# Attention and a gated MLP in one kernel on one core: q loaded with six tokens a partition, single-head scores at the start, a halved last store, and a new order

## The chip, the cores and the metric

The kernel runs on one core of a Trainium2 chip. The core has five engines that each work through a queue of their own in order: TensorE (PE in the profile, with PEld for its weight loads), VectorE (DVE), ScalarE (ACT), GpSimd (POOL) and SyncE (SP), which here only issues transfers. Sixteen DMA engines move the data. The engines wait for each other through semaphores. The metric is the time of one execution in device microseconds; lower is better.

## The reference

Grouped-query attention, whose output goes straight into a gated MLP with a spatial product. B = 8 batches, 16 q heads, 4 kv heads, 384 tokens, head size 64.

```python
scores = scale * np.matmul(q, k.transpose(0, 1, 3, 2))     # k, v repeated for 4 q heads each
attn = np.exp(scores - max) / sum
x = (attn @ v) -> (8, 384, 1024)
h = np.maximum(x @ w_in, 0.0)                              # 1024 -> 1024
u, v = h[..., :512], h[..., 512:]
v_n = (v - mean) / sqrt(var + 1e-6)                        # over the 512
v_s = w_spatial @ v_n (over tokens) + b_spatial
out = (u * v_s) @ w_out                                    # 512 -> 1024, float32
```

## The kernel before

All products run in fp16. The whole work is cut into pieces, and `lay_out` makes an operation of each: a cost, what it waits for, which buffers it uses, and the code that emits it. `Plan.run` goes through time with these costs and fixes the order in which each engine gets its instructions and which PSUM bank or SBUF slot a buffer takes. TensorE's order is written out by hand as words (`RAMP`, `PATTERN` for batches 2 to 7, `TAIL`); the order of the other engines follows from the plan. `LOADS` is the order of the first loads, and `CASTS` says which engine casts which of them to fp16.

The words, with b for the batch and gp for a pair of kv heads:

- `T.q.b.gp.t`, `T.k`, `T.ws`: transposes by TensorE (L425), for batches 0 and 1 and the spatial weights; VectorE copies the result to qT, kT or wsT (L389). From batch 2 on q and k are turned by DMA (L411).
- `S.b.n`: one tile of scores for a pair of kv heads, two products of 64 rows and 512 columns that run side by side (L595). ScalarE takes the exponential of both, 128 x 1024, into aT (L601). There are 18 such tiles a batch.
- `SM`: the sums of the exponentials (L634, with a matrix of ones). VectorE first adds the three key tiles (L620 and L623, two additions for each query tile), except in batch 0, where TensorE adds them. ScalarE makes the reciprocal by a logarithm and an exponential (L639, L642).
- `X`: the exponentials times v (L634); VectorE scales it into xT (L677, in batch 0 L728). Batch 0 does this in two groups of query tiles, the first alone and the other two together (`GROUPS`).
- `V.b.st`: x times the second half of w_in; relu, then statistics and normalisation on VectorE (L762, L763, L784), with ScalarE's square root in between (L773, L774).
- `SP`: the spatial product; VectorE adds the bias (L802).
- `U.b.m`: x times the first half of w_in; VectorE takes the relu and multiplies (L882). In batch 0 U goes by the groups of X too, with uT in between (L843, L856, L865).
- `O.b.c`: the output product, six chunks of 128 x 512 a batch. `OCOPY` says which engine copies the chunk from PSUM (L387 on ScalarE, L389 on VectorE). SyncE then stores a row block of 128 x 1024, in the last batch each 128 x 512 (L915, L922).
- `D`: a product of zeros that nobody reads. The words of before have none.

A product in a gap with sums or X is cut into four column strips of 32 (L358, mode C); otherwise it is whole (L354, mode F). Scores are a third mode. SyncE issues every load and store; a load waits for a free slot (six of `st32` for q, k, v; four of `big` for weights and for output) and for the transfer eight places ahead of it.

Partition p holds tokens 3p, 3p + 1 and 3p + 2 of each head, so that a load of q brings runs of 768 bytes:

```python
return x.rearrange("i (p t) d -> p i (t d)", t=NST)
dst = lambda tt=tt: e.out[b].rearrange("(p t) d -> p t d", t=NST)[:, tt, :]
```

Of the kernel before, what the change touches and what calls it, by code (L numbers as in the profile page):

```python
# [11 lines left out]
FP32 = mybir.dt.float32  # L12
# [33 lines left out]
class Plan:  # L46
# [13 lines left out]
    LOADING = 42.0  # L60

# [96 lines left out]
    def run(self, ahead):  # L158
# [17 lines left out]
        while left:  # L176
            progress = True
            while progress:
                progress = False
                for e in engines:  # L180
# [7 lines left out]
                    for o in ready:  # L188
# [8 lines left out]
                        if e == "PE":  # L197
                            t = self.fetch(o, t)
                            cost = self.clocked(o, t)
                        if o.lock:  # L200
                            t = max(t, locked)
                            locked = t + o.cost
# [52 lines left out]
    "T.q.0.0.1 T.k.0.0 T.q.0.0.0 S.0.8 S.0.1 S.0.2 S.0.6 S.0.0 T.k.0.1 T.q.0.1.0 S.0.5 T.q.0.1.2 "  # L255
    "T.q.0.1.1 S.0.4 S.0.3 S.0.7 T.q.0.0.2 S.0.9 SM.0.1.0.0 SM.0.0.0.0 S.0.16 T.ws.0 S.0.17 "
    "T.ws.1 S.0.15 T.q.1.0.2 T.q.1.0.1 S.0.12 S.0.10 T.q.1.0.0 T.k.1 S.0.11 S.0.14 X.0.1.0.0 "
    "X.0.0.0.0 S.1.0 S.1.4 X.0.1.1.1 S.1.6 X.0.1.1.0 S.0.13 SM.0.1.1.0 T.q.1.1.2 S.1.3 T.q.1.1.1 "
    "T.q.1.1.0 SM.0.0.1.0 S.1.1 S.1.5 X.0.0.1.1 X.0.0.1.0 V.0.0 S.1.16 S.1.2 S.1.8 V.0.2 V.0.1 "
    "S.1.7 S.1.10 S.1.9 U.0.0.0 U.0.1.1 SP.0.3 SP.0.2 S.1.13 SP.0.0 S.1.11 SP.0.1 X.1.0.1.0 "  # L260
    "S.1.15 S.1.12 S.1.17 U.0.1.0 S.1.14 X.1.0.0.0 X.1.0.0.1 SM.1.0.0 O.0.1 X.1.1.0.0 SM.1.0.1 "
    "SM.1.1.0 O.0.0 X.1.1.0.1 X.1.0.1.1"
)
PATTERN = (
    "SM.-1.1.1 S.0.3 O.-2.2 S.0.0 S.0.1 S.0.4 X.-1.1.1.1 X.-1.1.1.0 O.-2.1 O.-2.3 S.0.7 S.0.2 "
    "S.0.6 O.-2.4 V.-1.1 S.0.5 S.0.8 S.0.10 V.-1.2 V.-1.0 S.0.15 S.0.17 S.0.9 O.-2.5 X.0.0.0.0 "
    "SM.0.0.0 U.-1.2 U.-1.1 SP.-1.2 S.0.13 S.0.16 SP.-1.1 SP.-1.0 SP.-1.3 U.-1.3 S.0.12 S.0.14 "
    "S.0.11 U.-1.0 X.0.0.1.0 SM.0.0.1 X.0.0.1.1 O.-1.0 X.0.0.0.1 SM.0.1.0 X.0.1.0.0 X.0.1.0.1"
)
TAIL = (  # L270
    "SM.7.1.1 X.7.1.1.1 X.7.1.1.0 O.6.4 O.6.2 V.7.0 V.7.2 V.7.1 U.7.0 U.7.2 O.6.5 O.6.3 SP.7.1 "
    "SP.7.0 U.7.1 SP.7.3 SP.7.2 U.7.3 O.6.1 O.7.5 O.7.1 O.7.3 O.7.2 O.7.4 O.7.0"
# [3 lines left out]
def words():  # L276
# [21 lines left out]
GROUPS = ((0,), (1, 2))  # L298
PIECE = {1: 0.195, 2: 0.342, 3: 3 * (S / 2400.0 + 0.0025)}
OCOPY = ("ACT", "ACT", "DVE", "DVE", "ACT", "DVE")  # L300
LOADS = (
    "0q1", "0q0", "0k0", "0q3", "0k1", "0q2", "ws", "wi12", "1q1", "wo2", "wi01", "wi10", "1q0",
    "1k", "wi11", "0v", "wi13", "wi02", "1q3", "wi00", "wi03", "wo3", "wo1", "1q2", "1v", "wo0",
)
CASTS = {
    "0k0": ("DVE",), "0k1": ("POOL",), "0q0": ("DVE", "ACT", "DVE"),
    "0q1": ("POOL", "POOL", "POOL"), "0q2": ("POOL",), "0q3": ("POOL",), "1q0": ("DVE",),
    "1q1": ("DVE",), "1q2": ("POOL",), "1q3": ("DVE", "DVE", "POOL"), "wi10": ("POOL", "POOL"),
    "wi11": ("DVE", "DVE"), "wi12": ("DVE", "DVE"), "wi13": ("POOL", "DVE"),
    "wi00": ("POOL", "ACT"), "wi01": ("DVE", "DVE"), "wi02": ("POOL", "POOL"),  # L310
    "wi03": ("ACT", "ACT"), "wo0": ("POOL", "ACT"), "wo1": ("ACT", "ACT"),
    "wo2": ("DVE", "DVE"), "wo3": ("ACT", "ACT"),
}


def lay_out(e, seq, ocopy=OCOPY, loads=LOADS, casts=CASTS, groups=GROUPS):

# [53 lines left out]
    def idling(w):  # L371

        pb = Buf("ps", "idle", banks=1)

        def f():
            e.nc.tensor.matmul(ap(pb)[:, 0, :], e.idle16[:, 0:P], e.idle16, start=True, stop=True)

        f.__name__ = f"idle_{w[2]}"
        plan.op("PE", mm(512), f, after=[c_dve], uses=[pb], rank=at[w], mode="F", code=2)
# [22 lines left out]
    def loading(o, i, name, rank, size, after=(), uses=(), cost=0.45):  # L402
        def f():
            e.nc.sync.dma_start(o(), i())

        f.__name__ = name
        return plan.op("SP", cost, f, after=after, uses=uses, rank=rank, late=0.75, size=size)
# [11 lines left out]
    def turned(word, n, src, dst, need, uses, eng="DVE"):  # L419
# [3 lines left out]
        def f():  # L423
            for m in range(n):
                e.nc.tensor.transpose(half16(pb)[:, m * P : (m + 1) * P], src(m), e.ident16)  # L425
# [4 lines left out]
        return copying(eng, n * 64, dst, lambda: half16(pb)[:, 0 : n * P], f"turned_{word}", psum=True,  # L430
                       after=[o], uses=[pb] + uses[1:], rank=-1.0)

    def prepare(b, rank, bias, after=()):

# [7 lines left out]
        for n, key in enumerate(keys):  # L442
            def src(key=key):
                if key[0] == "q":
                    x = e.q[b, key[1] * G : (key[1] + 1) * G]
                else:
                    x = {"k": e.k, "v": e.v}[key[0]][b]
                    if len(key) == 2:
# [6 lines left out]
            ld[key] = loading(lambda u=u, i=i: ap(u)[:, 0 : i * 192].rearrange("p (i n) -> p i n", i=i),  # L455
                              src, f"load_{key}_{b}", at_, 0.32 * i, after, [u])
# [13 lines left out]
        for gp in range(NGP):  # L470
            q16[gp] = Buf("q16", f"q16_{b}_{gp}")
            qT[b, gp] = Buf("qT", f"qT_{b}_{gp}")
            for z in range(2):
# [3 lines left out]
                for m, eng in enumerate(hs):  # L477
# [3 lines left out]
                            "p (t h u d) -> p u h t d", t=NST, h=G, u=2)[:, z, :, m * n : (m + 1) * n],  # L481
                        lambda key=key, m=m, n=n: ap(raw[key]).rearrange(
                            "p (h t d) -> p h t d", h=G, t=NST)[:, :, m * n : (m + 1) * n],
# [27 lines left out]
        for gp in range(NGP):  # L511
            if by_pe:
                for t in range(NST):
                    qT_op[b, gp, t] = turned(
# [41 lines left out]
    def weights_spatial(eng, bias):  # L556
        w16, bu = Buf("k16", "ws16"), Buf("rec", "b_row")
        u = Buf("big", "ws32")
# [492 lines left out]
```

## Time and profile before

| | us |
|---|---|
| median of 3 runs | 249.76 (248.67, 250.67, 249.76) |
| the profiled execution | 248.71 |
| its span, first to last instruction | 246.9 |
| TensorE busy | 231.3 |
| ScalarE busy | 195.1 |
| VectorE busy | 190.5 |
| GpSimd busy | 52.2 |

The profile is of one execution, whose own time is 248.71; the span leaves out what lies before its first and after its last instruction. Busy time of TensorE includes the modelled ends of products that overlap, so it is not the time at its peak rate. In the chain of work each piece has its start, its length, the engine, the tile it writes and the line; "x16" is the number of instructions merged into it. In the timeline a bracket gives the idle time before a group and what ended it. Lines such as L389 and L425 are helpers: the tile tells the pieces apart.

### The profile page before, as it was taken

To read this page: it belongs to the slowest core of one execution; us is meant where nothing else is said; L and a number is where in the kernel's file an instruction comes from. 1 tells how busy PE (TensorE), PEld (TensorE's weight loads), DVE (VectorE), ACT (ScalarE), POOL (GpSimd) and SP (SyncE) were. 2 spreads that over 40 slices of the span, in tenths; PEclk is the share of its full clock that TensorE was granted. 3 is DMA by queue.
4 is the path that set the end of the run, shared out by engine and by line. 5 is a ranking of instruction groups with operands and counts; after the bars stand their busy time and mean duration, and the time that the engine had idled before them with its cause. 6 is when DMAs were issued, how large, how long until landed. Compare 5 with 4: busy or idle time off the path is not lost.

```text
span 246.9 us, 7793 instructions
## 1 busy us (share of the span) xinstructions
PE 231.3 (94%) x3352; PEld 116.5 (47%) x3352; DVE 190.5 (77%) x353; ACT 195.1 (79%) x276; POOL 52.2 (21%) x70
## 2 busy tenths in 40 slices
PE   0868999999999999999999999999999999999992
PEld 0434557454355435554355435444455445555650
DVE  1366599998789877997789877987799767984850
ACT  2699999979887999599987999599977998672011
POOL 2514654103506220225004320405000000000000
PEclk9999999999999999999999999999999999999999
DMA  6999999719999088933968097923920042000345
GB/s 207 362 349 354 363 343 343 144 38 310 262 273 304 3 194 198 305 108 125 206 215 254 5 225 184 323 72 146 187 85 3 3 170 88 3 3 3 131 164 222
DMA packets 56083, 44.94 MB, mean 182 GB/s; under 512 B 25072, under 2 KB 49904, under 8 KB 56048
## 3 DMA queue, kind: packets, MB, share of 16 engines
q1 hardware_dynamic: 56048, 44.44, 62.1%
q8 instruction: 26, 0.43, 0.7%
q14 instruction: 9, 0.07, 0.1%
HBM read 25.95 MB, written 12.58 MB: 156 GB/s over the span
## 4 chain that ended last, share of the span: by engine, by line
PE 78%; ACT 8%; DVE 4%; issue 1%
PE ps L358 28%; PE ps L354 26%; PE ps L634 13%; PE ps L595 11%; ACT aT L601 7%; DVE sm L623 1%; DVE spb L802 1%; DVE v_n L784 1%; DVE gT L882 0%; DVE sm L620 0%; ACT rec L642 0%; ACT rec L639 0%; DVE gT L856 0%; PE ps L425 0%; DVE uT L843 0%
## 5 line engine op out<-in xcount | busy, mean ns | idle before, releaser
L601 ACT ACTIVATE aT<-ps 128x1024 f16<-128x1024 f32 x144 | 139.1, 1050 | 19.5 <-PE ps L595 18.8
L595 PE MATMUL ps<-qT,kT 64*128 64x512 f16 x288 | 43.9, 389 | 2.4 <-ACT aT L601 1.6
L634 PE MATMUL ps<-aT,v 128*32 128x384 f16 (+2 forms) x864 | 39.1, 309 | 0.0
L354 PE MATMUL ps<-w_in,xT 128*128 128x512 f16 x160 | 36.7, 380 | 0.0
L620 DVE TENSOR_TENSOR sm<-aT 128x1024 f16<-128x1024 f16 x42 | 34.5, 826 | 1.7 <-ACT aT L601 1.3
L358 PE MATMUL ps<-w_out,gT 128*32 128x512 f16 x576 | 35.1, 380 | 0.0
L623 DVE TENSOR_TENSOR sm<-sm,aT 128x1024 f16<-128x1024 f16 x42 | 30.3, 734 | 5.4 <-ACT aT L601 5.4
L391 POOL CAST q<-q 128x768 f16<-128x768 f32 (+1 forms) x31 | 29.8, 974 | 19.4 <-DMA q<-in_q_dram 19.0
L677 DVE TENSOR_TENSOR xT<-ps,rec 128x384 f16<-128x384 f32 x56 | 28.5, 551 | 6.1 <-PE ps L634 2.2
L358 PE MATMUL ps<-xT,w_in 128*32 128x384 f16 x704 | 31.3, 327 | 0.0
L634 PEld LDWEIGHTS <-v 128*32 128x32 f16 x864 | 21.1, 97 | 13.5 <-issue 3.7
L595 PEld LDWEIGHTS <-kT 64*128 64x128 f16 x288 | 11.6, 95 | 28.2 <-issue 22.5
L354 PEld LDWEIGHTS <-xT 128*128 128x128 f16 x160 | 15.0, 98 | 20.7 <-issue 3.9
L762 DVE BATCH_NORM_STATS2 stats<-v_r 128x6 f32<-128x512 f32 x24 | 16.6, 693 | 10.0 <-ACT v_r L758 9.9
L358 PEld LDWEIGHTS <-w_in 128*32 128x32 f16 x704 | 18.2, 97 | 11.8 <-issue 2.5
L389 DVE COPY osb<-ps 128x512 f32<-128x512 f32 x27 | 18.5, 689 | 6.1 <-PE ps L358 4.2
L387 ACT COPY osb<-ps 128x512 f32<-128x512 f32 x21 | 12.6, 599 | 12.3 <-PE ps L358 11.9
L391 POOL CAST k<-k 128x384 f16<-128x384 f32 x15 | 7.7, 541 | 68.4 <-DMA k<-in_k_dram 68.4
L358 PEld LDWEIGHTS <-gT 128*32 128x32 f16 x576 | 15.0, 96 | 14.9 <-issue 2.5
L758 ACT ACTIVATE v_r<-ps 128x512 f32<-128x512 f32 x21 | 12.8, 612 | 7.4 <-PE ps L358 4.3
L639 ACT ACTIVATE rec<-ps 128x384 f32<-128x384 f32 (+2 forms) x32 | 16.5, 518 | 2.5 <-PE ps L634 1.6
L642 ACT ACTIVATE rec<-rec 128x384 f32<-128x384 f32 (+2 forms) x32 | 17.2, 548 | 0.6
(55 smaller groups left out, 205.0 us busy)
## 6 DMA issues: line engine op xcount, KB each, us to landing
q<-in_q_dram SPq DMA_DIRECT2D x32, 384.0 KB, 7.0
out_dram<-osb SPq DMA_DIRECT2D x21, 512.0 KB, 3.1
w_in<-in_moe_w_in_dram SPq DMA_DIRECT2D x8, 512.0 KB, 8.4
v<-in_v_dram SPq DMA_DIRECT2D x8, 384.0 KB, 7.1
k<-in_k_dram SPq DMA_DIRECT2D x7, 384.0 KB, 4.2
w_out<-in_moe_w_out_dram SPq DMA_DIRECT2D x4, 512.0 KB, 7.9
out_dram<-osb SPq DMA_DIRECT2D x6, 256.0 KB, 3.3
k<-in_k_dram SPq DMA_DIRECT2D x2, 192.0 KB, 4.7
```

What stands on the lines that cost most here:

```text
L354: e.nc.tensor.matmul(out, weights, moving, start=start, stop=stop)
L358: e.nc.tensor.matmul(out[c], weights[:, c], moving, start=start, stop=stop)
L389: e.nc.vector.tensor_copy(o, i)
L391: e.nc.gpsimd.tensor_copy(o, i)
L595: e.nc.tensor.matmul(ap(u)[:, half, :], ap(kT[b])[lo:hi, gp, kt, :], ap(qT[b, gp])[lo:hi, qt].rearrange("p h n -> p (h n)"), start=True, s ...
L601: e.nc.scalar.activation(ap(aT[b, gp])[:, qt, kt].rearrange("p (u n) -> p u n", u=2), ap(u), AF.Exp, scale=scale)
L620: e.nc.vector.tensor_tensor(total(), exps(0), exps(1), ALU.add)
L623: e.nc.vector.tensor_tensor(total(), total(), exps(2), ALU.add)
L634: e.nc.tensor.matmul(dst[32 * i : 32 * (i + 1)], weights(t), moving(t, i), start=(n == 0), stop=(n == len(ts) - 1))
L642: e.nc.scalar.activation(ap(rc)[:, 0:n], ap(rc)[:, 0:n], AF.Exp, scale=-1.0)
L677: e.nc.vector.tensor_tensor(ap(xT[b])[:, gp * 4 + z * 2 + jj, :], ap(xb)[:, 0, 0:S], ap(rc)[:, 0:S], ALU.mult)
L762: e.nc.vector.bn_stats(stats, ap(r))
```

## The change

- q is loaded with six tokens a partition: 64 partitions hold one head and the other 64 the next, so that a run is 1536 bytes. The columns of qT come in another order, and the scores read them back by heads, in eight runs of 64 columns. The spatial weights and their bias are arranged to fit; the weights come in two loads of 64 partitions, into a buffer of their own.
- An output row block is now two stores of 64 partitions, one for each parity of the token.
- The first k goes out on ScalarE's queue, ahead of the load of the activation table.
- The scores of the first query tile and the first pair of kv heads (`HALVES`) are made for each kv head alone: transposes of 64 rows, one product and an exponential of 128 x 512.
- U of batch 0 is made whole, as in the other batches. The relu of its first V tile is on ScalarE (`OPTS` r0). In batch 1, the second pair of heads (p11) gets one addition on VectorE, and TensorE adds the third key tile.
- The last chunk of the output is made in two halves of 256 columns, both copied by ScalarE; of each half one store goes by SyncE's queue and one by ScalarE's.
- Four of six output copies a batch are on VectorE instead of three. New words with 26 idle products of 256 columns, a new order of loads, new casts, and two settings of the plan (`BACKLOG`; how many loads it looks ahead).

```diff
 RAMP = (
+    "D.0.0 D.0.1 ... D.0.15 T.k.0.0 T.q.0.0.0.0 D.0.16 T.q.0.0.2 S.0.2.0 S.0.1.0 T.q.0.0.1 S.0.14 D.0.17 "
+    "T.q.0.0.0.1 S.0.6 D.0.18 S.0.1.1 S.0.2.1 S.0.0.1 S.0.0.0 S.0.13 D.0.19 T.k.0.1 D.0.20 "
...
+HALVES = ((0, 0, 0),)
+SPLIT = 0
-OCOPY = ("ACT", "ACT", "DVE", "DVE", "ACT", "DVE")
+OCOPY = ("DVE", "ACT", "DVE", "ACT", "DVE", "DVE")
 LOADS = (
-    "0q1", "0q0", "0k0", "0q3", "0k1", "0q2", "ws", "wi12", "1q1", "wo2", "wi01", "wi10", "1q0",
-    "1k", "wi11", "0v", "wi13", "wi02", "1q3", "wi00", "wi03", "wo3", "wo1", "1q2", "1v", "wo0",
+    "0q0", "0q1", "0q2", "0k1", "0q3", "0v", "1q0", "ws", "1q1", "1k", "wi11", "wi13", "wi02",
+    "wi12", "wi10", "wi03", "wi01", "wi00", "1q3", "1q2", "wo2", "wo3", "wo0", "wo1", "1v",
 )
 CASTS = {
+    "0k0": ("ACT",), "0k1": ("DVE",), "0q0": ("DVE",), "0q1": ("POOL", "DVE", "ACT"),
...
+OPTS = {"p10": 2, "p11": 1, "r0": 1, "r1": 0, "r2": 0}
...
-                    x = e.q[b, key[1] * G : (key[1] + 1) * G]
+                    return e.q[b, key[1] * G : (key[1] + 1) * G].rearrange(
+                        "(i a) (p t) d -> (a p) i (t d)", a=2, t=2 * NST)
...
+            first = b == 0 and key == ("k", 0)
...
+                              eng="ACT" if first else "SP")
+            if first:
+                plan.op("ACT", 1.3, e.table, rank=-8.0)
...
-            for half in range(2):
+            for m, half in enumerate(us):
                 lo, hi = half * D, (half + 1) * D
                 e.nc.tensor.matmul(
-                    ap(u)[:, half, :], ap(kT[b])[lo:hi, gp, kt, :],
-                    ap(qT[b, gp])[lo:hi, qt].rearrange("p h n -> p (h n)"), start=True, stop=True,
+                    ap(u)[:, m, :], ap(kT[b])[lo:hi, gp, kt, :],
+                    ap(qT[b, gp])[lo:hi, qt].rearrange("p (j i) (a n) -> p (i a) j n", j=2, a=2),
+                    start=True, stop=True,
...
+        def store(tt, osb, c, need, both=False):
+            for j in range(2):
+                def f(j=j):
+                    dst = e.out[b].rearrange("(p t j) d -> t j p d", t=NST, j=2)[tt, j]
+                    (e.nc.scalar if both and j else e.nc.sync).dma_start(dst[:, c], ap(osb)[j * D : (j + 1) * D, c])
...
+                if last and c == SPLIT:
+                    cuts = [(("O", b, c, m), hf * 512 + 256 * m, 256) for m in range(2)]
```

## The prediction

> **What bounds the kernel now.** I read the windows first, then the chain that ended last, then the timeline of the first 30 us and of the last 10, then the DMA issues. The windows give, for each stretch, its length and the busy us of PE, PEld, DVE, ACT and POOL, then TensorE's granted clock, DMA share and GB/s:
>
> ```profile
> 6.00:30.00 24.00, 19.55 (x350) 11.59 (x351) 13.31 (x34) 21.64 (x28) 10.13 (x16) 1.00 1.07 357
> 30.00:62.90 32.90, 32.49 (x418) 17.25 (x409) 31.30 (x59) 30.18 (x45) 11.53 (x16) 1.00 0.84 241
> ...
> 118.00:145.60 27.60, 27.60 (x373) 13.05 (x370) 23.20 (x41) 24.07 (x35) 6.32 (x7) 1.00 0.66 181
> ```
>
> A batch in the steady middle takes 27.60 us and TensorE is busy in all of it; VectorE has 4.4 us and ScalarE 3.5 us to spare. From 30 us on TensorE is busy all but 0.4 us. Before 30 us it is not: ScalarE is the one without gaps there (its idle part of the 24 us is the start). The chain, in order of time, says the same:
>
> ```profile
> 18.77 8.35 ACT aT L601 x10
> ...
> 32.34 1.73 PE ps L358 x32
> 34.07 0.76 PE ps L595 x6
> 34.83 3.56 PE ps L354 x16
> ...
> 220.49 21.86 PE ps L358 x447
> 242.35 0.02 issue
> 242.37 0.58 ACT osb L387
> ```
>
> Up to 28.9 us the chain runs through the exponentials (L601); the first product with w_in (V of batch 0, the x32 at 32.34) opens TensorE's stretch, and 210.0 us later, at 242.35, the last output product ends. In between the chain leaves TensorE only for short stretches (54.5 to 59 us on ScalarE, 72 to 80 on VectorE). So three things make the span of 246.9: when V of batch 0 can start, how much TensorE has to do from there, and what follows the last product. The start, by the timeline (start, length, engine):
>
> ```profile
> 4.40 1.08 POOL L391 CAST q<-q 128x256 f16<-128x256 f32 x3 [3.10 <-DMA q<-in_q_dram]
> 5.54 0.49 DVE L389 CAST q<-q 128x256 f16<-128x256 f32 x2 [4.36 <-DMA q<-in_q_dram]
> 6.15 0.36 DVE L389 CAST k<-k 128x384 f16<-128x384 f32 x1
> 8.36 8.36 ACT L601 ACTIVATE aT<-ps 128x1024 f16<-128x1024 f32 x9 [2.41 <-PE ps L595]
> ```
>
> The first exponential waits for the third transfer (k, at 6.1 us) and 2.2 us of cast, transpose, copy and score. Nine exponentials in 8.36 us make 0.93 each.
>
> **The change, part by part.** *The start.* k of the first pair goes out on ScalarE's queue beside the first q on SP's, and a score of one kv head needs one q transfer, not two. No row shows a load on ScalarE's queue. The first q lands 3.6 us after its issue (0.73 to 4.34), and the next 384 KB 1.18 later; k's 192 KB and the first q sharing those engines make k land near 4.3, the first q near 4.8, the second near 5.9. On ScalarE the k cast (0.4, as its 256-wide q cast at 5.54) is then done at 4.8. But the first score (S.0.2.0) stands on TensorE behind the transpose T.q.0.0.2, which needs ScalarE's cast from the second q (5.9 + 0.4 = 6.3), and its own q copy stands on VectorE behind a cast from the second q too (5.9 + 0.25, then 0.43 of copy = 6.6). Score 0.4: first exponential at 7.05. Bounds: 6.3 if the second q comes 0.75 sooner, 8.36 if k gains nothing.
>
> *ScalarE up to the last exponential of batch 0.* Now: 21 exponentials (three belong to batch 1) and four small ones of the reciprocals (1.1 us by their starts), 8.36 to 28.86. After: the instruction order has 6 halves, 15 whole ones of batch 0 and one of batch 1, and the same four. A half has no row; the 128x512 logarithm at 28.48 lets the next start 0.48 later, which I take (bounds 0.465, half of 0.93, and its whole length 0.86). 6 x 0.48 + 16 x 0.93 + 1.1 = 18.9, so the last one ends at 7.05 + 18.9 = 25.95, 2.9 earlier. This needs ScalarE to be fed: q, k for the second pair land near 8.6 and are cast on POOL by 9.5, and are wanted at 12.7; q of batch 1, behind which scores queue on TensorE, is cast by 17.5 and wanted at about 18.
>
> *From there to V.* Now 28.86 to 32.34. After, the order puts 96 narrow products (SM and X, as the x24 of 0.84 and x48 of 1.43 in the chain: 2.9), two score pairs (0.55) and four transposes (0.25) there: 3.7, so V starts at 29.7 instead of 32.34: 2.65 us gained. V's last weight chunk (wi10) stands 8.1 MB down the queue. Now 6.8 MB are in at 24.0 and 11.0 MB at 35.6, so with eight quicker q loads ahead of it (0.12 each) it is in near 26.7 and cast by POOL at 28: 1.7 us of cover; if that goes, V is late by what exceeds it. U's last chunk (wi00, 10.9 MB) is in near 34, cast at 35.2, wanted at 36.5.
>
> *TensorE from V on.* The lists of instructions differ by little: one more score pair behind V (0.22: the x6 of 0.76 less the x2 of 0.32, halved), four more transposes (0.22), eight more sums of batch 1 because one of its two additions is dropped (8 x 0.041 = 0.33, from 64 products in 2.77 and 32 in 1.47), U of batch 0 in four whole pieces instead of tiles (-0.08), and two more changes of mode (0.1 each): 0.9 us given back. After the first score of batch 2 work and mode changes are the same to 0.02 us. The 26 idle products stand ahead of V where TensorE waits anyway (it idles or stalls over half of 6 to 30 us); uncovered they are 26 x 0.11 = 2.8.
>
> *VectorE and ScalarE behind V.* VectorE is busy 31.3 of 32.9 us there and loses three additions (0.6 each by their starts), one relu (0.6) and some 1.2 of U's gating, and gains an output copy; ScalarE loses three weight casts (0.55 each) and gains a relu. TensorE is the bound there, so nothing is counted; at most the 0.4 us that TensorE idles. In every later batch one output copy moves from ScalarE to VectorE: 0.6 into its 4.4 spare. Nothing is counted; if VectorE were late, X's normalisation is next, and TensorE's V behind it.
>
> *Loads and stores.* q in runs of 1536 bytes instead of 768: at 1536 the bias took 0.52 per 192 KB against 0.6 for q; hidden, since by the above V and U do not wait for a load. Every store becomes two of 64 partitions: 27 more issues of 0.33 to 0.36 on SP, which waits most of the time for output copies.
>
> *The tail.* The last chunk is copied in two halves on ScalarE and stored by both queues. Now: product ends 242.35, copy 0.6, issue at 242.98, landed 245.90, then 1.0 to the end of the span.
>
> ```profile
> 238.77 4.54 SPq L915 DMA_DIRECT2D out_dram<-osb  x6
> ...
> 242.37 0.58 ACT L387 COPY osb<-ps 128x512 f32<-128x512 f32 x1 [0.28 <-PE ps L358]
> ```
>
> The half copy takes about 0.35 to 0.4 (256-wide rows) instead of 0.58, and the last bytes are fewer: -0.3. The six 256 KB stores now land 0.61 to 0.63 us apart whatever their issue: the tail is at the rate of its stores. No row has a store from 64 partitions. Bounds: the same bytes at the same rate (-0.5), or each at half the rate: 1.23 for 256 KB, six of them and the 512 KB before them, +3.7 (about +5 if the first is as late as now). I take the row, full rate, as all rows have.
> The Trainium skill, SBUF — State Buffer, section "Door 1: The DMA port swizzle", speaks against it: partitions 0 to 63 reach eight of sixteen ports, 196 GB/s against 328 at 1 MiB, and by "Can I just issue two DMAs to hit both halves?" a pair does not make it up. No run here shows it yet; by that the tail would be the second bound.
>
> **Sum.** -2.65 + 0.9 - 0.3 = -2.05 us. The profiled execution took 248.71 (span 246.9 and 1.8 around it), so 246.6. The runs shown have their median at 249.76, 1.05 higher, with 2 us between them; 1% (2.5 us) is about what a measurement can tell from no change.
>
> **Rivals.** *Stores at half rate* (the tail): ramp -1.75, tail +3.7 to +5: 250.7 to 252.0, slower than before. For it: the tail already runs at the store rate. Against: each transfer still goes over all engines. It decides from the point where a pair of 128 KB stores takes over 0.86 us, the time of a chunk's product; in the middle the DMA share of 0.66 hides it. *Scores read q in eight runs of 64 columns*: 144 pairs; the sum turns at 14 ns a pair and reaches 1% slower at 32; at twice the 0.216 of a pair it is +31, 278. Against: X's products (L634) read three runs of 128 with no loss. I price it at 252 or more. *The ramp gives nothing*: ScalarE starts early but starves, since scores queue behind transposes that wait for casts, and V starts at 32 with 0.9 us more to do: 249.3. *The ramp gives more*: the first exponential at 6.3 and the 0.4 us of idle gone: 245.4.
>
> **How the numbers follow.** Forecast 0.50; ramp more 0.14; half-rate stores 0.18; ramp nothing 0.11; slow score reads 0.07. Range: from 244.4 (the ramp's best less the tail's lower bound and some) to 250.9, which takes in the first rival's near end; beyond it lie its far end and slow reads. The forecast's own range is 245.2 to 247.9. Faster by over 1%: the ramp-more case and most of the forecast, 0.55; within 1%: the rest of it, the ramp without gain and most of the store rival, 0.33; slower 0.12.
>
> **What would show it.** First exponential near 7, no gap of ScalarE over 0.4 us up to 26, V near 29.7, the first score of batch 2 near 52.4 (now 54.1), 27.6 us a batch, last landing 3.2 us after the last product. Wrong if V is later than 31, if a score pair takes over 0.22, or if the last stores land over 0.8 us apart per chunk.

## The result, and the profile after

The changed kernel takes 250.86 us (median of 20 runs, 249.46 to 252.87) where the kernel before takes 249.47 beside it (20 runs, 248.29 to 250.79). The ratio is 1.0066, 95% interval 1.0041 to 1.0092: slower by 0.7%, 1.6 us (1.4 us by the medians). The forecast was 246.6. The profiled execution has a span of 248.5 (246.9 before). A ratio is of the executions within 1.5% of the fastest of the same kernel; below, this leaves out four of the twelve of the whole stores, and elsewhere one or none.

The windows of the changed kernel, with the columns of before (length, then busy us of PE, PEld, DVE, ACT, POOL, then clock, DMA share, GB/s):

```profile
6.00:30.00 24.00, 20.84 (x404) 12.20 (x402) 13.38 (x29) 22.65 (x33) 13.30 (x19) 1.00 1.08 343
30.00:60.00 30.00, 29.96 (x322) 13.99 (x319) 25.99 (x49) 27.36 (x40) 12.10 (x18) 1.00 0.86 232
107.73:135.25 27.52, 27.52 (x383) 13.14 (x380) 23.22 (x42) 23.55 (x33) 6.33 (x7) 1.00 0.72 188
```

ScalarE gained 1 us of work between 6 and 30 us, and TensorE still has no gap from 30 us on. A batch takes 27.5 instead of 27.6. The first exponentials, by the timeline (start, length, engine; the bracket is idle time and what ended it):

```profile
4.96 0.51 ACT L394 CAST k<-k 128x384 f16<-128x384 f32 x1 [2.41 <-DMA k<-in_k_dram]
6.01 0.41 ACT L394 CAST q<-q 128x256 f16<-128x256 f32 x1 [0.54 <-DMA q<-in_q_dram]
7.38 6.72 ACT L623 ACTIVATE aT<-ps 128x512 f16<-128x512 f32 x10 [0.96 <-PE ps L616]
```

The first starts at 7.38 instead of 8.36. The last part of the chain of work up to V of batch 0 (the x8 of 1.73):

```profile
15.16 10.70 DMA q<-in_q_dram
25.86 0.02 issue
25.88 0.57 DVE q L396
26.45 0.05 issue
26.50 0.40 PE ps L432 x4
26.90 0.32 PE ps L616 x2
27.22 2.83 PE ps L657 x96
30.05 0.54 PE ps L616 x4
30.58 0.33 PE ps L432 x4
30.91 1.73 PE ps L361 x8
```

By its first product V starts at 30.75 instead of 32.17, and the chain came there through a load of q of batch 1 that landed at 25.86 (TensorE was idle for 0.23 us before the transposes that waited for it). The last product ends at 240.49 instead of 242.33: 1.84 us were gained up to there. Then comes the end, by the timeline of the queues:

```profile
236.01 9.34 SPq L865 DMA_DIRECT2D out_dram<-osb  x14
...
239.72 1.19 ACT L394 COPY osb<-ps 128x512 f32<-128x512 f32 x3 [2.01 <-PE ps L365]
240.61 1.22 ACTq L865 DMA_DIRECT2D out_dram<-osb  x2
```

SyncE issues 14 stores without a pause from 236.01 to 245.35, 0.47 to 0.66 us each and one of 0.99 (0.33 for most of before's). The last lands at 247.12, 6.6 us after the last product (3.6 before). The last pairs of 128 KB landed 1.1 to 1.5 us apart. From the last product to the end of the span are 8.0 us (248.48 less 240.49), where there were 4.6 (246.94 less 242.33). So 3.4 us were lost at the end and 1.8 gained before it. The same windows of the two kernels at the end, before first and after second:

```profile
240.00:242.00 2.00, 2.00 (x44) 1.03 (x36) 1.17 (x2) 0.49 (x1) 0.00 (x0) 1.00 0.78 285
242.00:244.00 2.00, 0.33 (x8) 0.00 (x0) 0.00 (x0) 0.68 (x2) 0.00 (x0) 1.00 1.04 389
```

```profile
240.00:242.00 2.00, 0.49 (x20) 0.20 (x8) 0.00 (x0) 0.91 (x3) 0.00 (x0) 1.00 0.86 247
242.00:244.00 2.00, 0.00 (x0) 0.00 (x0) 0.00 (x0) 0.00 (x0) 0.00 (x0) 0.91 0.95 250
```

The last two columns say it: from 242 to 244 us full or nearly full engines moved 389 GB/s before and move 250 now.

### The profile page after: what moved, and what is told of

It is laid out like the page before. It is cut to its first block, busy times and chain, and to the rows that moved or that the text cites. A ratio compares the mean times of both kernels' runs of the same rounds, so it can differ in the third digit from the quotient of the medians.

```text
span 248.5 us, 7929 instructions
## 1 busy us (share of the span) xinstructions
PE 235.4 (95%) x3413; PEld 117.7 (47%) x3413; DVE 187.8 (76%) x345; ACT 191.9 (77%) x273; POOL 57.2 (23%) x75
## 3 DMA queue, kind: packets, MB, share of 16 engines
HBM read 25.95 MB, written 12.58 MB: 155 GB/s over the span
## 4 chain that ended last, share of the span: by engine, by line
PE 86%; DMA 8%; SPq 1%; POOL 1%; ACT 0%; issue 0%; DVE 0%; POOLq 0%; ACTq 0%
PE ps L365 30%; PE ps L361 28%; PE ps L657 15%; PE ps L616 13%; DMA q<-in_q_dram 4%; DMA ws<-in_moe_w_spatial_dram 3%; SPq L411 1%; POOL ws L398 1%; ACT osb L394 0%; PE ps L432 0%; DVE q L396 0%; POOL b_tp L398 0%; POOLq L398 0%; ACTq L394 0%
## 5 line engine op out<-in xcount | busy, mean ns | idle before, releaser
L623 ACT ACTIVATE aT<-ps 128x1024 f16<-128x1024 f32 (+1 forms) x147 | 139.7, 1033 | 14.6 <-PE ps L616 14.4
L361 PE MATMUL ps<-w_in,xT 128*128 128x512 f16 x168 | 38.8, 379 | 0.0
L646 DVE TENSOR_TENSOR sm<-aT 128x1024 f16<-128x1024 f16 x42 | 32.5, 776 | 4.2 <-ACT aT L623 4.1
L365 PE MATMUL ps<-w_out,gT 128*32 128x512 f16 (+1 forms) x592 | 35.1, 373 | 0.0
L646 DVE TENSOR_TENSOR sm<-sm,aT 128x1024 f16<-128x1024 f16 x39 | 29.2, 752 | 5.4 <-ACT aT L623 4.9
L707 DVE TENSOR_TENSOR xT<-ps,rec 128x384 f16<-128x384 f32 x56 | 28.2, 548 | 4.4 <-PE ps L657 3.0
L398 POOL CAST q<-q 128x768 f16<-128x768 f32 (+1 forms) x28 | 26.6, 961 | 18.6 <-issue 10.0
L396 DVE COPY osb<-ps 128x512 f32<-128x512 f32 x33 | 22.6, 687 | 4.6 <-PE ps L365 3.1
L398 POOL CAST k<-k 128x384 f16<-128x384 f32 x14 | 10.1, 748 | 65.5 <-DMA k<-in_k_dram 61.6
L616 PEld LDWEIGHTS <-kT 64*128 64x128 f16 x288 | 11.5, 94 | 25.9 <-issue 19.4
L790 ACT ACTIVATE v_r<-ps 128x512 f32<-128x512 f32 x22 | 13.4, 611 | 8.9 <-PE ps L365 5.6
L834 DVE TENSOR_TENSOR spb<-ps,b_tp 128x384 f32<-128x384 f32 x32 | 17.1, 557 | 3.0 <-PE ps L365 2.5
L852 DVE SCALAR_TENSOR_TENSOR gT<-ps,spb 128x384 f16<-128x384 f32 x32 | 17.4, 551 | 0.2
```

The lines of the kernel that those rows point to most:

```text
L361: e.nc.tensor.matmul(out, weights, moving, start=start, stop=stop)
L365: e.nc.tensor.matmul(out[c], weights[:, c], moving, start=start, stop=stop)
L396: e.nc.vector.tensor_copy(o, i)
L398: e.nc.gpsimd.tensor_copy(o, i)
L616: e.nc.tensor.matmul(ap(u)[:, m, :], ap(kT[b])[lo:hi, gp, kt, :], ap(qT[b, gp])[lo:hi, qt].rearrange("p (j i) (a n) -> p (i a) j n", j=2, ...
L623: e.nc.scalar.activation(ap(aT[b, gp])[:, qt, kt, us[0] * 512 : (us[-1] + 1) * 512].rearrange("p (u n) -> p u n", n=512), ap(u), AF.Exp, s ...
```

## The experiments

Two readings of the end were put against each other. Theory I: a 64-partition store is long to issue, and two of them (1.2 us) exceed the 0.86 us of a chunk's product. Theory P, the prediction's first rival: its transfer goes at half the rate. Ratios are to the kernel before, run beside it on the same chip; "the end" is the time from the last product to the end of the span in the profiled execution. (Two more theories came up with the traces of the first runs: C, of TensorE's clock, and W, of the loads of the spatial weights.)

### The end

**Stores on two queues.**

```diff
-store(tt, osb, slice(c0, c0 + n), cp[-1:], n < 512)
+store(tt, osb, slice(c0, c0 + n), cp[-1:], True)
```

> The changed kernel with one edit: in the last batch the second store of every pair (64 partitions) goes out on ScalarE's queue, not only those of the halved chunk. Theory I (the queue that issues is the bound: a store from 64 partitions occupies SyncE 0.55 to 0.6 us, two of them more than the 0.86 us of a chunk's product): one store a chunk per queue fits, the last landing comes 3.5 us or less after the last product instead of 6.6, the span ends 4.5 to 5.0 us after it instead of 8.0, and the time falls by 3.0 to 3.5 us, to 247.5 to 248 (ratio to the kernel before 0.992 to 0.996). Theory P (64 partitions reach half the ports, the transfers themselves are the bound): the landings stay as far apart, the span still ends 7.5 to 8.0 us after the last product, 250 to 251 us.

Measured: 249.96, ratio 1.0000 (0.9969 to 1.0031); the end 6.1 us. About half of the loss came back (1.9 of 3.4 us), which neither theory said. The windows of the end:

```profile
242.50:244.50 2.00, 0.44 (x16) 0.15 (x8) 0.00 (x0) 0.86 (x2) 0.00 (x0) 1.00 0.92 296
244.50:246.50 2.00, 0.00 (x0) 0.00 (x0) 0.00 (x0) 0.37 (x1) 0.00 (x0) 1.00 0.91 296
```

The engines stay nearly full, at 296 GB/s instead of 250.

**Row pairs in the kernel before.**

```diff
-e.nc.sync.dma_start(dst()[:, c], ap(osb)[:, c])
+for j in range(2): r = slice(64 * j, 64 * (j + 1)); e.nc.sync.dma_start(dst()[r, c], ap(osb)[r, c])
```

> The kernel before with one edit: each of the last batch's six 128x512 stores is two, of partitions 0 to 63 and 64 to 127, both on SyncE; nothing else changes. Theory I: each takes 0.55 to 0.6 us to issue instead of 0.33, the twelve take about 7 us from 238.8, and the span ends 2.5 to 3.5 us later: 252 to 253 us, with pairs landing 1.1 to 1.3 us apart, each 2 to 2.7 us after its issue. Theory P: the issues stay at 0.33 to 0.36 and the pairs land 1.2 us apart because the transfers pile up, landing later and later after their issue (3 us growing to 6); also +3 to +5 us. A third reading, that only the number of stores counts (0.33 each): under +0.5 us.

Measured: 253.53, ratio 1.0140 (1.0093 to 1.0187); the end 8.4 us, 3.8 more than before. From the third on the issues are 0.54 to 0.60 long and each store lands 2.3 to 2.4 us after its issue, as theory I has it; but the windows show full engines at about half the rate (202 to 209 GB/s):

```profile
245.00:247.00 2.00, 0.00 (x0) 0.00 (x0) 0.00 (x0) 0.00 (x0) 0.00 (x0) 0.57 0.97 209
```

In the trace's records of single packets a packet of 2048 bytes takes 162 ns (median) here and 86 in the kernel before. A pair of 128 KB at 205 GB/s is 1.28 us, and two issues with their gaps are 1.27: this run can't part the theories.

**Column pairs in the kernel before.** As above with `c` cut into two of 256 columns and all 128 partitions.

> The kernel before with one edit: each of the last batch's six 128x512 stores is two of 256 columns, all 128 partitions (runs of 1024 bytes), both on SyncE. As many stores as with the pairs of rows. If it is the 64 partitions that make an issue long: 0.33 us each, and the end moves by 0 to +0.7 us (the runs of 1024 bytes may cost the transfer something): 249.5 to 250.3. If any second store costs 0.55 to 0.6 us to issue: +2.5 to +3.5 us.

Measured: 250.97, ratio 1.0047 (1.0017 to 1.0078); the end 6.1 us. Issues back to back take 0.38 to 0.45 and come 0.49 apart, and the engines are not full:

```profile
245.00:247.00 2.00, 0.00 (x0) 0.00 (x0) 0.00 (x0) 0.00 (x0) 0.00 (x0) 1.00 0.84 274
```

So many small stores do run into the issue, at a milder price (1.5 us at the end), and it looks different: a DMA share of 0.71 to 0.84.

**The same half on both queues.** The run that parts the theories: as the stores on two queues, but both stores of a pair read partitions 0 to 63.

```diff
-ap(osb)[j * D : (j + 1) * D, c]
+ap(osb)[slice(0, D) if both else slice(j * D, (j + 1) * D), c]
```

> The stores on two queues (first run) with one edit: in the last batch the second store of every pair, on ScalarE's queue, reads partitions 0 to 63 again instead of 64 to 127 (so half of the last batch's rows hold the other half's values; the bytes and the issues are the same). Theory I (issue is the bound): nothing changes, the span ends 6 to 6.3 us after the last product, DMA share 0.9 at 290 to 310 GB/s. Theory P (each half of the partitions is served at half the rate, and two queues help because both halves are then read at once): both queues now pull on the same half, 2048-byte packets take 160 ns or more throughout, the rate stays at 200 to 210 GB/s with the engines full, and the span ends 8 to 9.5 us after the last product, 252 to 253.5 us.

Measured: 252.24, ratio 1.0074 (1.0044 to 1.0103), against 1.0000 with both halves; the end 7.6 us instead of 6.1.

```profile
243.00:245.00 2.00, 0.00 (x0) 0.00 (x0) 0.00 (x0) 0.38 (x2) 0.00 (x0) 0.85 1.00 201
245.00:247.00 2.00, 0.00 (x0) 0.00 (x0) 0.00 (x0) 0.03 (x1) 0.00 (x0) 0.50 0.99 197
```

As many queues, issues and bytes, and the rate falls from 296 to 199 GB/s with the engines full. Theory I fails here: the transfer from one half of the partitions is the bound, at half of the 389 GB/s of whole stores. What the issue alone would cost on one queue stays open, since both limits come to 1.3 us a pair.
The Trainium skill, SBUF — State Buffer, section "Door 1: The DMA port swizzle", has this: 64 partitions reach half of the ports. The trace agrees (about 200 against 389 GB/s). Its section "Can I just issue two DMAs to hit both halves?" says that two transfers, one from each half, gain only 6% and serialize. Here they gained more: 296 GB/s on two queues against 199 for the same half twice, and 250 on one queue. The measurement decides.

The changed kernel itself, with one queue, shows both limits. Its store of 236.52 us took 0.59 us to issue while the engines were 0.03 busy (236 to 237 us), so these issues are long without full engines too. And the engines, 0.95 busy from 242 to 244 us, are not full after that, while SyncE still issues until 245.35:

```profile
244.00:246.00 2.00, 0.00 (x0) 0.00 (x0) 0.00 (x0) 0.00 (x0) 0.00 (x0) 0.50 0.66 152
246.00:248.00 2.00, 0.00 (x0) 0.00 (x0) 0.00 (x0) 0.00 (x0) 0.00 (x0) 0.50 0.29 61
```

The rate is thus shown to be a limit, and the issue stands beside it; no run divides the loss between them.

**Two queues, output copies on VectorE.**

> The changed kernel with the last batch's stores on both queues, as in the first run, and its output copies on VectorE (one 256-wide half stays on ScalarE), so that ScalarE does little else than issue. Theory I: ScalarE's issues no longer wait behind its copies and its copies no longer behind issues; the span ends 4.6 to 5.2 us after the last product (6.2 with the copies on ScalarE), 247.8 to 248.6 us, ratio to the kernel before 0.992 to 0.997. Theory P: no better than the stores on two queues, 249.6 to 250.2.

Measured: 250.96, ratio 1.0015 (0.9983 to 1.0047); the end 6.2 us, against 6.1 with the copies on ScalarE. So ScalarE's copies were not what kept the two queues from more.

**Whole stores, other rows.**

```diff
-dst = e.out[b].rearrange("(p t j) d -> t j p d", t=NST, j=2)[tt, j]     # two stores of 64 partitions
+dst = e.out[b].rearrange("(p t) d -> t p d", t=NST)[tt]                 # one of 128
```

> The changed kernel with one edit: every pair of 64-partition stores is one store of 128 partitions on SyncE, in all batches, written to the rows as the kernel before writes them (so the rows of the output stand in another order; all bytes are stored). Theory I (issue time of the 64-partition stores is the tail's loss): 0.33 us an issue, the span ends 4.3 to 4.8 us after the last product instead of 8.0, and the median falls by 3 to 3.6 us against the changed kernel, to 247.3 to 248 (ratio to the kernel before 0.991 to 0.995). If something else in the tail costs the time (the order of the last products, the halved chunk): 249 or more.

Measured: 247.68, ratio 0.9875 (0.9838 to 0.9911); the end 3.6 us. At the end alone that is 4.4 us less than in the changed kernel (8.0 less 3.6, by the profiles). In all it is 3.1 us by the spans of the two profiles (248.5 less 245.3; this one lost 1.3 us ahead of its last product, in two batches of 28.1 and 28.2 us), 3.8 by the medians of all executions (1.0056 against 0.9905) and 4.8 by the ratios (1.0066 / 0.9875 = 1.019). The pairs of stores are what made the changed kernel slower; without them it is faster than before.

**The halved last chunk alone**, in the kernel before.

> The kernel before with one part of the change alone: its last output chunk (O.7.0) in two halves of 256 columns, both copied on ScalarE, the first stored by SyncE and the second by ScalarE's queue, all 128 partitions each. The prediction took 0.3 us for it; the whole-store run ended 3.55 us after its last product against 4.57 in the kernel before. By that: -0.8 to -1.1 us, ratio 0.995 to 0.997; by the prediction's term -0.3, 0.998 to 1.0. If the stores ahead of it bound the end anyway: 1.0.

Measured: 250.14, ratio 1.0028 (1.0005 to 1.0050); the end 4.75 us against 4.61. In the kernel before the halving brings nothing. Where the 1.0 us between 4.6 and 3.6 comes from no run tested: in the kernel before the first store of the end landed 4.4 us after its issue (3.1 with the whole stores), and its last few packets started as late as 241.5, when most had gone by 240; instruction fetches of 16 and 8 KB pass at 238.9, 240.3 and 240.9.

### Whole stores with every row in its place

**One store, two strides**: the 128 partitions go to rows of DRAM in two strides.

> The changed kernel with one edit: every pair of 64-partition stores is one store from all 128 partitions whose rows in DRAM go in two strides; in the last batch all of them on SyncE (the halved chunk's two halves as well). Theory I, with the partitions as the cause of the long issue: 0.33 to 0.4 us each, the span ends 4.3 to 5.0 us after the last product instead of 8.0, 247.3 to 248.3 us. If the two strides and not the partitions make an issue long (0.6 to 1.1 us): the span ends 5 to 6.5 us after the last product, 248.5 to 249.5. Theory P: as with the partitions as the cause, since all 128 are in one transfer, but with the issues of the changed kernel unexplained.

Measured: 372.79, ratio 1.493 (1.487 to 1.499). A window of the end, where nothing but stores runs:

```profile
340.00:350.00 10.00, 0.00 (x0) 0.00 (x0) 0.00 (x0) 0.00 (x0) 0.00 (x0) 0.50 0.13 51
```

A share of 0.13 is two engines of sixteen (0.13 x 16 = 2.1): the outer dimension of the transfer had two entries. SyncE's issues of 256 KB grow to 4.9 us and more, and everything behind them on that queue is late.

**Rows in order by the gating**: VectorE writes gT's columns in row order.

> The changed kernel with two edits that give every store 128 partitions and the right rows: the gating on VectorE writes gT's columns in the order of the rows (columns 64 apart in its inputs go 6 apart in its output), so that a chunk of 128 rows stands on 128 partitions in order and one store on SyncE takes it. Theory I: as the whole stores with other rows: the span ends 3.5 to 4.0 us after the last product, ratio to the kernel before 0.985 to 0.991 (246.3 to 248). What could spoil it: the gating, 32 times 0.47 to 0.56 us, slower by its output's step of 12 bytes; VectorE has 4 us a batch to spare, so up to 0.9 us each is hidden; from there V and the output products come late, 0.3 to 1 us a batch.

Measured: 272.27, ratio 1.089 (1.085 to 1.093). The end is 3.8 us, as hoped, but the gating (columns: busy us, mean ns) went from the first row, of the changed kernel, to the second:

```profile
L852 DVE SCALAR_TENSOR_TENSOR gT<-ps,spb 128x384 f16<-128x384 f32 x32 | 17.4, 551 | 0.2
```

```profile
L853 DVE SCALAR_TENSOR_TENSOR gT<-ps,spb 128x384 f16<-128x384 f32 x32 | 45.7, 1454 | 0.2
```

The 0.9 us more of each was to be hidden and is not: the gating stands in the chain of work (13.9% of it from 120 to 151 us), and a batch takes 31 us.

**Rows in order by the moving operand**: U reads xT with a step of 64 columns (128 bytes).

> The changed kernel with 128-partition stores and the right rows in another way: the spatial weights and their bias are loaded in the order of the rows (one load of 128 partitions instead of two of 64), and U's products read xT with a step of 64 columns, so that the gating writes in order without a step. If TensorE reads a moving operand with a step at full rate: the tail ends 3.5 to 4 us after the last product, 1q1 lands 1.3 us earlier, ratio to the kernel before 0.980 to 0.990 (245 to 247.5). If a step of 128 bytes halves the rate: U's 128 products of 384 columns a batch cost 5.2 us more each batch, 285 to 290 us in all.

Measured: 399.47, ratio 1.602 (1.595 to 1.609). U's row, in the changed kernel and here:

```profile
L365 PE MATMUL ps<-xT,w_in 128*32 128x384 f16 x704 | 32.2, 326 | 0.0
```

```profile
L365 PE MATMUL ps<-xT,w_in 128*32 128x384 f16 x704 | 136.9, 891 | 0.0
```

**The last two batches in the old layout.** q of batches 6 and 7 as before, with a second set of spatial weights for them.

```diff
+if key[0] == "q" and b >= B - 2: x = e.q[b, ...]; return x.rearrange("i (p t) d -> p i (t d)", t=NST)
+lb = loading(lambda: e.ws32, lambda: e.moe_w_spatial.rearrange("(p a) s -> p a s", a=NST), ...)
+(e.nc.scalar if act else e.nc.sync).dma_start(dst[:, c], ap(osb)[:, c])
```

> The changed kernel, but batches 6 and 7 load q with three tokens a partition as the kernel before does, so that their output rows stand on 128 partitions and are stored whole (the last chunk's second half on ScalarE's queue); for them the spatial weights are loaded, cast on GpSimd and transposed by DMA a second time near 115 to 130 us, in the other order, beside the work of batch 3. All rows are right. Theory P: no store of 64 partitions is left in the tail, the span ends 3.5 to 4.8 us after the last product instead of 8.0, ratio to the kernel before 0.984 to 0.992 (245.8 to 248). It would be slower if the second set of spatial weights collides with the loads of a batch (590 KB and 1.2 MB of transposes beside 27 us that have a DMA share of 0.7): up to 1 us.

Measured: 248.33, ratio 0.9911 (0.9876 to 0.9945): faster than both kernels. The end is 4.0 us, at the full rate:

```profile
240.00:242.00 2.00, 2.00 (x44) 0.95 (x36) 1.28 (x2) 0.32 (x1) 0.00 (x0) 1.00 1.00 380
```

### The start

The executions of the changed kernel lie 3.4 us apart (2.5 before), in groups: ten up to 250.5, six from 251.2 to 251.8, four from 252.7. The first runs above have the same instructions as the changed kernel up to V, and yet V started at 30.75 there and at 33.27 in the stores on two queues. The transposes point to the reason. By the timeline, in the profile of the changed kernel, of the same half on both queues, and of the stores on two queues:

```profile
10.46 0.33 PE L432 MATMUL ps<-ident,k 128*128 128x128 f16 x3
...
15.06 0.40 PE L432 MATMUL ps<-ident,ws 128*128 128x128 f16 x4 [0.30 <-POOL ws L398]
```

```profile
9.47 0.64 PE L432 MATMUL ps<-ident,q 128*64 128x128 f16 x4
...
12.65 0.33 PE L432 MATMUL ps<-ident,k 128*128 128x128 f16 x3
```

```profile
13.05 0.53 PE L432 MATMUL ps<-ident,k 128*128 128x128 f16 x3
...
13.58 1.06 PE L432 MATMUL ps<-ident,q 128*128 128x128 f16 x8
...
17.50 0.51 PE L432 MATMUL ps<-ident,ws 128*128 128x128 f16 x6
```

One transpose follows the next after 107 ns at first and after 56 ns later. The full speed came between 4.4 and 5.6 us in the first (V at 30.75), between 9.7 and 12.7 in the second (31.64), between 15.1 and 17.5 in the third (33.27). In the whole stores it came before 5.6 (30.68), in the copies on VectorE and the old layout between 15 and 17.6 (33.25, 33.33). The clock column shows 1.00 for the start of the changed kernel and of the stores on two queues alike; only the distance of the products shows the difference. In the profile of the kernel before full speed came between 10.8 and 12.1 us (V at 32.17). That V moves with it is what these profiles have in common; what the unprofiled executions of the changed kernel did is not recorded, so that the groups of their times come from it is likely and not shown.
The Trainium skill, TensorE: Matmul & The Clock Gate, section "Part 1: The HAM clock gate", describes such a gate: half speed until a free-running window of 3.4 us was busy, so that the moment differs from run to run. The trace agrees in the two speeds, 107 and 56 ns, and in a moment that differs from run to run. It does not agree with the half microsecond to either side that the section gives for it: here the moments lie some 10 us apart, in a start of mixed work, and the measurement decides.

**No idle products.**

> The changed kernel without its 26 idle products. Theory C: in the profiles the clock opened at 5.5 us (V of batch 0 at 30.7) or only at about 16 (V at 33.3), as the idle products fell into its windows; without them it opens at 10 to 16 as in the kernel before, V starts at 32 to 33.5, no execution is under 250.8, the median is 251.2 to 252.5 and the spread narrower. If the idle products only cost TensorE's time: the median falls by 0.3 to 1 us, to 249.9 to 250.6. The tail stays at 8 us.

Measured: 256.27, ratio 1.0237 (1.0203 to 1.0271), 1.7% or 4.2 us worse than the changed kernel. V starts at 34.06, the last product ends at 245.10. Full speed came between 13.4 and 16 us and was gone again at 24. The idle products are worth more than theory C said. About 1.4 us of it lies behind V: from V to the first score of batch 2 it is 24.0 us, against 22.6 in the changed kernel.

**Six more idle products at the start.**

> The changed kernel with six more idle products behind the first sixteen (1.3 us at half speed, which fill the wait before the first transpose). Theory C (TensorE's clock opens after a stretch of work that must fill a window whose phase differs from execution to execution; in the profile of the changed kernel it opened before 5.5 us, in that of the stores on two queues only at 16, and V of batch 0 came 2.5 us later): the clock opens early in more of the executions, the median falls by 0.5 to 1.2 us to 249.7 to 250.3, and the spread of the times shrinks from 3.4 us. If the idle products do nothing for the clock, or the first transpose is made late by them: 250.8 to 251.2. The tail stays at 8 us.

Measured: 252.10, ratio 1.0070 (1.0038 to 1.0101): no gain. In the profile full speed came at 6.9 us, was gone again at 17.9, and V started at 32.32.

**Twenty more later**, with the old layout in the last two batches.

> The last two batches in the old layout, as in the run before, and the ten idle products that stand between the first score and V of batch 0 tripled (twenty more, 0.11 us each at full speed and 0.21 at half speed, where TensorE mostly waits for exponentials). Theory C: they fill windows that were not busy enough, the clock opens earlier in the executions in which it opened only at about 16 us, and the median falls by 0.5 to 1 us, ratio to the kernel before 0.985 to 0.990. If the windows miss for another reason, the products only stand in the way at half speed (up to 4 us of them): 0.992 to 1.0.

Measured: 250.10, ratio 1.0010 (0.9974 to 1.0047), against 0.9911 without them. Full speed came at 5.4 us and V still started only at 32.11: the products stood in the way even at full speed (the chain of work goes through 1.8 us of them between 7.9 and 11.5 us).

**Idle products in the kernel before**, with the halved chunk.

> The kernel before with the halved last chunk as in the run beside it, and eleven idle products of 512 columns ahead of its first transpose (4.7 us at half speed, from 1.1 us to 5.8). In the kernel before TensorE runs at half speed up to 10.4 to 16 us. Theory C: the clock opens at about 6 in about half of the executions and V of batch 0 starts up to 1 us earlier there: 0.2 to 0.8 us less than the run beside it, ratio 0.992 to 0.996. If the old start waits for its loads and ScalarE and not for TensorE: the same as the run beside it within 0.2 us.

Measured: 250.47, ratio 1.0044 (1.0021 to 1.0067), against 1.0028 for the run beside it: nothing. Full speed came by 6.0 us, and V started at 32.23, where it started at 32.17 with full speed between 10.8 and 12.1: that early the old start waits for other things. It does depend on the speed when that comes late: with the same start, full speed came only after 16 us in the profiles of the halved chunk and of the column pairs, and V started at 33.80 and 33.46.

**The first k on SyncE.**

> The changed kernel with its first k load back on SyncE's queue, ahead of the first q, as one part undone. The first k lands near 4.0, the first q near 5.0, the second near 6.1, a later one each by 0.1 to 0.3 us than now; first exponential at 7.4 to 7.7 (now 7.4). By the prediction's own step the second q is what the first score waits for (through the transpose ahead of it), so the part should be worth 0 to 0.3 us: median 250.7 to 251.3. If the part is worth what the change claims of it, the first exponential goes to 8 or later and the median to 251.5 or more.

Measured: 252.38, ratio 1.0090 (1.0058 to 1.0122), against 1.0066. The intervals overlap, so what the part is worth in time (0.24%, 0.6 us, by the two ratios) is not resolved. In the profile the second q landed at 7.14 (6.1 expected; 5.99 in the changed kernel) and the first exponential started at 8.38, where the second reading had it; in the changed kernel it started at 7.38, and in the profiles of the same start whose full speed came late at 7.7 to 7.9. So the part gains 0.5 to 1.0 us at the first exponential, more than 0 to 0.3.

**Spatial weights later.**

> The changed kernel with the two loads of the spatial weights (64 partitions each, 1.4 to 1.75 us for 295 KB, half the rate of the other loads) moved from before 1q1 to behind the last w_in chunk that V needs, and their two transposes on TensorE from before the first X to behind V. Theory W (they delay q of batch 1 and with it the scores and the clock-open ramp): q of batch 1 (1q1) lands 3.2 us earlier (16.5 us), V of batch 0 starts 0.6 to 1.2 us earlier than in a profile whose clock opens alike, median 249.7 to 250.3. If the ramp is TensorE's and ScalarE's anyway: within 0.3 us of the changed kernel, 250.6 to 251.2.

Measured: 259.87, ratio 1.037 (1.032 to 1.042). 1q1 landed at 17.30 (19.78 in the changed kernel, 16.5 expected), but the planner let three chunks of w_in into the place that the spatial weights had filled, while q's slots were taken; the last q of batch 1 was issued at 21.31 and landed at 31.52 instead of 25.86, and V started at 38.74. This tells of the order of loads and nothing of theory W.

**Spatial weights on two queues.**

> The changed kernel with the second of the two spatial-weight loads (64 partitions each) on ScalarE's queue, so that both halves of the partitions are read at once. Theory W (half of the partitions get half the rate; one behind the other they hold up all later loads): the two land together in 1.7 to 2.0 us instead of 3.25, q of batch 1 (1q1) lands 1 to 1.5 us earlier (18.3), and in executions whose clock opens early V starts up to 1 us earlier: median 0.3 to 0.8 us lower, 250.0 to 250.6. ScalarE loses 0.6 us to the issue while it waits for the first q. If the loads are not what the ramp waits for: within 0.3 us, 250.6 to 251.2.

Measured: 253.56, ratio 1.0121 (1.0084 to 1.0159). 1q1 landed at 18.50 (18.3 expected), but ScalarE's half went out at 1.31, ahead of most of q of batch 0, whose second load landed at 6.57 instead of 5.99 and third at 8.82 instead of 7.05. It cost more at the front than it gave behind. That the two loads of 64 partitions run at half the rate (1.50 and 1.75 us for 288 KB each, packets of 1536 bytes 124 ns against 68) is plain; that they cost V time was not shown.

## Why the prediction was wrong

**The term that failed is the end.** The prediction set -0.3, took full rate for stores from 64 partitions "as all rows have", and let 27 more issues on SyncE pass at 0.33 to 0.36 us each. The end measured +3.4: the nearly full engines moved 250 GB/s instead of 389 (199 with one half of the partitions alone), and the issues took 0.47 to 0.66 us, one of them 0.99. Whole stores in the same kernel end at 3.6, so the pairs cost 4.4; the rest of the tail gave 1.0, and in the kernel before the halved chunk alone gave none of that. Taking the nearest row was the wrong choice here: every row of a store was one of 128 partitions, so no row spoke of the other kind, and what the pairs cost lies between the two bounds of half the rate (+3.7, about +5). Of the three signs of being wrong that the prediction named, one came: the last pairs landed 1.1 to 1.5 us apart, not under 0.8.

**The rival was right in its price, and its mechanism is shown as one of two.** "Stores at half rate" was priced at +3.7 to +5 at the end and 250.7 to 252.0 in all, from the point where a pair of 128 KB takes over 0.86 us. It takes about 1.0 on one queue with overlap (256 KB at 250 GB/s) and 1.28 without; the time is 250.86. It had a chance of 0.18. Its case against, that each transfer still goes over all engines, is no argument: the engines were 0.93 to 1.00 busy at 197 to 250 GB/s. It priced neither the long issues nor the 1.0 us gained elsewhere in the tail, so its total is met in part by luck.

**Up to the last product the sum was right by luck, and its terms were not.** Forecast -2.65 + 0.9 = -1.75, measured -1.84 in the profiled execution. V came 1.4 us earlier, not 2.65; from V to the first score of batch 2 0.4 us were given back, not 0.9; and from there to the last product 0.8 us were gained where nothing was counted (27.47 a batch for 27.59). The last was not tested. V came at 30.75 and not at 29.7. The first exponential was 0.33 us late (7.38 for 7.05). The last one of batch 0 ended 0.8 late (26.74 for 25.95), since ScalarE waited on the way: 1q1, of the q of batch 1 that was to be cast by 17.5, landed at 19.78, TensorE was idle for 0.93 us before its transposes at 20.6, and ScalarE for 0.38 at 22.39. From there to V it took 4.0 and not 3.7, with transposes of another q of batch 1, cast at 26.45, ahead of the X products. The half exponentials came 0.48 apart, as forecast, and the whole ones 0.90, not 0.93: the prediction's division took in the end of the last one.

**The idle products were costed at nothing, with TensorE's waits as cover.** That taking them out costs 4.2 us was missed, because the prediction never asked at what speed TensorE runs in the start: it priced one at 0.11 us, and the first sixteen come 0.21 apart. In profiles with the same start V lies between 30.7 and 33.3 as full speed comes early or late, so the profiled execution may flatter the start by up to 2.5 us against others of the same kernel.

**The other rivals.** Score pairs took 0.22, so reading q in eight runs of 64 columns costs nothing. The start gave neither nothing nor more than forecast.

**A reading.** The prediction has the chain of work leave TensorE only from 54.5 to 59 and from 72 to 80 us. In the profile of before it also leaves it from 38.7 to 47.2, for ScalarE and VectorE. TensorE was busy through nearly all of that, and no term of the sum rests on it.

## What to carry to other kernels

A layout that saves on a load can be paid again at the store that has to undo it: look at what the last transfers of a kernel become, since nothing hides them. Where no row of a trace shows the kind of transfer that a change introduces, the pessimistic bound is a forecast of equal standing; and DMA share beside GB/s tells a slow transfer (full engines, low rate) from a slow issue (engines not full). Profile a start more than once, by the distance of equal products, before a gain in it is counted.

## What the runs showed of the hardware that was not expected

- Two queues that read the two halves of the partitions reach 296 GB/s, the same half twice 199, whole stores 380 to 389.
- An outer dimension of two put a 128-partition store on two engines, at 51 GB/s. The Trainium skill, DMA: Bandwidth & Descriptors, section "Why a DMA increments its semaphore by 16 and not by 1", derives the number of engines from that dimension; the trace agrees.
- A step of 12 bytes in the fp16 output of VectorE's gating made it 1454 ns instead of 551, and a step of 128 bytes in TensorE's moving operand made a product of 384 columns 891 ns instead of 326, while runs of 64 columns cost nothing.
- A 64-partition store takes 0.47 us to issue, and 0.59 right behind another, even when the engines are idle (236.0 to 237.1 us of the changed kernel); one of 128 partitions in rows of 2 KB takes 0.33.
- Equal transposes came 107 ns apart in one stretch of a start and 56 in another while the profile's clock column showed 1.00 for both.
